# Gate rows' transposes moved behind the product with v, into its banks, and the gate products of two half-batches put in one turn

## Chip, cores and metric

One Trainium2 chip, one of its cores. The metric is the device time of one execution in microseconds (us); lower is better. The kernel is one launch that holds attention and the mixture of experts.

## What is computed

Causal attention in a window of 64 positions, followed by a mixture of experts that picks one expert for each token and skips the tokens whose skip score isn't positive:

```python
scores = scale * np.matmul(q, k.transpose(0, 1, 3, 2))        # B=8, H=8, S=576, D=64
rel = pos[:, None] - pos[None, :]
scores = np.where((rel >= 0) & (rel < 64), scores, -1000000000.0)
attn = softmax(scores)
out = np.matmul(attn, v)                                      # [8, 8, 576, 64]
x = out.transpose(0, 2, 1, 3).reshape(B * S, H * D)           # [4608, 512]
do_compute = x @ w_skip > 0
logits = x[do_compute] @ w_gate                               # 8 experts
e_idx = argmax(logits); gate_w = softmax(logits)[e_idx]
y = gate_w * (relu(x @ w1[e_idx]) @ w2[e_idx])                # 512 -> 1024 -> 512
out = x, with x + y in the rows of do_compute
```

## The kernel before

**Attention tiles.** The 4608 tokens are worked in 36 tiles of 128 rows, each of two blocks of 64 positions. A batch has nine blocks; four tiles take eight of them, and after each second batch a ninth tile takes the two last blocks of both (a "tail tile", tile number 8 of each nine). A block looks at its own 64 positions and at the 64 before. A half-batch `n` (0 to 15) is four blocks, two tiles; its v with the columns around it is the buffer `vm`, whose first tile is `first_of[n] = 9*(n//4) + 2*(n%4)`.

**A turn.** The order of the instructions is written out by hand: a loop `for t in range(NT - 1)` issues one turn for each tile, and each engine works through its own queue in that order. Turn t starts the loads of its table, then issues:
- `score(t + 1)`: on PE four matmuls of the band mask (L238) and 16 small products of q and k (L252) into `ps` (the trace counts each product of fp32 operands twice);
- the gate work of its table `gate_at`: `gate_v` multiplies `vT` (v transposed) with the gate's and the skip's weights `wg`, so that the logits come out of the attention's own product (PE L336, `pw`, four matmuls; ACT L338 copies it to `vw`); a turn later `gate_vt` turns `vw` back with two transposes (PE L344, `pk`), ACT L356 copies them beside v in columns 65 to 74 of `vm`, and POOL L357 copies the upper half of `vm` to the slot of the block before. `gate_tail` and `gate_tail_t` do the same for the tail tiles with one transpose;
- `soften(t)`: DVE takes the maximum (L271) and subtracts it (L272), ACT the exponential (L277);
- `tile_out(t - 2)`, and in it `av_tile`: the product with v (PE L388, 16 matmuls, 74 columns a head: 64 of v, the row sum, nine of the gate) into two PSUM banks `av`; then DVE takes the reciprocal of the sums (`r`, L399, L400), writes `x` (L401) and the gate's columns `lh` (L407);
- `transpose_p(t - 1)`: eight PE transposes `pt` (L285), which ACT copies to `ptm` (L286) for the product of the next turn;
- `lower`: ACT copies of one block of `vm` (L364).

So a product of turn t is that of tile t - 2, and a half-batch's `vm` is first used in turn `first_of[n] + 2`.

**PSUM.** `pw`, `pk` and `pt` take turns in two banks (tag "t", `bufs=2`). `ps` has two buffers of two banks, `av` one of two banks (`bufs=1`), of which the product takes columns 0 to 295 of each.

**Routing beside it.** From the gate's columns of eight or six tiles at a time, generators that `routes(1)` steps three times a turn work out the lists of tokens for each expert. Most of it is POOL: the logits' sums (`lh`, `lg`, L468, L469), the choice (`gd` to `gohb`, L484 to L502), the rank in the expert's list (`gs`, `gds`, `rows`, L505, L537 to L539) and the lists' entries as one-hot rows (`xg`, L599 to L611). Two small products on PE, the ranks' (L517, L520) and the lists' (L560), are written into the `av` banks behind the product's columns, from column `PRAT` = 320 on; DVE reads the ranks' (`gds`, L530). POOL's copies of L357 stand in the same queue.

**Loads.** SP issues them in program order, a few turns ahead: `load_v(n)`, `vT` and then `vm` of the same half-batch, in turn `first_of[n] - 4` (L296, L302); q and k at `first_of[n] - 5` (L210, L211); the attention's outputs `x` go out between them (L426).

**Experts.** After the last tile, tokens are gathered by an indirect DMA (L732) and the experts' products (L918 to L920) run to the end.

Of the kernel before, what the change touches and what calls it, by code (L numbers as in the profile page):

```python
# [8 lines left out]
F32 = mybir.dt.float32  # L9
# [11 lines left out]
P = 128  # L21
# [29 lines left out]
AHEADQ, AHEADV = 5, 4  # L51
# [17 lines left out]
XN = max(n for _, n, _ in ITEMS)  # L69
NEG = -float(2**36)  # L70
VW = 64 + 1 + 9
PRAT = 320


def token_tiles():
# [69 lines left out]
def window_attention_moe(ctx: ExitStack, tc, a, out):  # L145
# [147 lines left out]
    def load_vT(n):  # L293
        b, g = divmod(n, 2)
        vT = vtp.tile([P, 4, 256], F32, name="vT")
        nc.sync.dma_start(vT, a["vT"][b, g])  # L296
        vTs[n] = vT
# [8 lines left out]
            nc.gpsimd.memset(vm[:64, 0], 0.0)  # L306
        vms[n] = vm

    def load_v(n):
        load_vT(n)  # L310
        load_vm(n)

    vTs, vws = {}, {}

    def load_v_tail(m):
# [23 lines left out]
        return vw  # L339

    def gate_t(vw, nt):
        pk = psum.tile([P, nt, P], F32, name="pk", tag="t", bufs=2, padded_shape=[P, 4, P])
        for j in range(nt):
            nc.tensor.transpose(pk[:, j], vw[:, j * P : j * P + P], ident)  # L344
        return pk.rearrange("p n (h c) -> p n h c", c=16)[..., 0:9]

    def gate_v(n):
        vws[n] = gate(vTs.pop(n), 2)

    def gate_vt(n):  # L350

        b, g = divmod(n, 2)
        vm = vms[n]
        pg = gate_t(vws.pop(n), 2)
        w = vm.rearrange("p (j z) h c -> p j z h c", z=2)
        nc.scalar.copy(w[:, :, 1, :, 65:74], pg)  # L356
        nc.gpsimd.tensor_copy(w[64:, :, 0], w[:64, :, 1])  # L357
        for j in range(2):
            vs[9 * (n // 4) + 2 * (n % 4) + j] = [vm[:, 2 * j], vm[:, 2 * j + 1]]

# [8 lines left out]
    def gate_tail_t(m):  # L369
        vt, vw = vms["t", m]  # L370
        pg = gate_t(vw, 1)
        for z in range(2):
            nc.scalar.copy(vt[64:, z, :, 65:74], pg[64 * z : 64 * z + 64, 0])
        vs[9 * m + 8] = [vt[:, 0], vt[:, 1]]

    def tail_lower(m, z):
# [2 lines left out]
    def av_tile(t, lh, sums, av=None):  # L379
        blks = tiles[t]  # L380
        ptm, win = pts.pop(t), vs.pop(t)
        x = xp.tile([P, D], F32, name="x", bufs=XPB)
        if av is None:
            av = pav.tile([P, 2, 512], F32, name="av")
        banks["av"] = av
        for h in range(8):
            for hf in range(2):
                nc.tensor.matmul(  # L388
                    av[64 * hf : 64 * hf + 64, h // 4, (h % 4) * VW : (h % 4 + 1) * VW],
                    ptm[:, (h % 2) * 4 + h // 2, 64 * hf : 64 * hf + 64],  # L390
                    win[hf][:, h],
                    start=True,
                    stop=True,
                )
        if sums:
            sums()
        r = sm.tile([P, 2, 4], F32, name="r")
        src = av[:, :, : 4 * VW].rearrange("p z (h c) -> p z h c", c=VW)
        nc.vector.tensor_scalar(r, src[..., 64], 1e-9, None, op0=ALU.add)  # L399
        nc.vector.reciprocal(r, r)  # L400
        pace[0] = nc.vector.tensor_tensor(  # L401
            x.rearrange("p (z h c) -> p z h c", z=2, c=64),
            src[..., 0:64],
            r.unsqueeze(3).to_broadcast([P, 2, 4, 64]),
            op=ALU.mult,
        )
        nc.vector.tensor_tensor(  # L407
            lh.rearrange("p c (z h) -> p z h c", z=2),
            src[..., 65:74],
            r.unsqueeze(3).to_broadcast([P, 2, 4, 9]),  # L410
            op=ALU.mult,
        )
        if sums:
            sums()
        stores.append((x, blks))
        while len(stores) > (SDELAY if t < NT - 6 else 0):
            store()
# [362 lines left out]
    def listing():  # L780
        step(later, held2)

    grp = [0, 0, None]
    heads = [sum(GRP[:i]) for i in range(len(GRP))]

    def tile_out(t, av=None):
        if t in heads:
            n = GRP[heads.index(t)]
            grp[:] = [t, n, xp.tile([P, n, 9, H], F32, name="lh")]
        t0, n, lh = grp  # L790
        behind = None
        if held[0] == "sums" and held[1] >= WAIT.get(t0, 2):
            behind = sums
        elif held2[0] == "lists" and held2[1] >= LWAIT:
            behind = listing
        av_tile(t, lh[:, t - t0], behind, av)
        progress[0] = t + 1
        if t + 1 == t0 + n:
            late.append(route(t0, n, lh))
# [337 lines left out]
    with tc.manual_schedule():  # L1137
# [17 lines left out]
        def when_at(t, f, n):  # L1155
            at.setdefault(max(t, 0), []).append((f, n))

        gate_at, lower_at = {}, {}
        for n in range(NG):
            if n >= 2:  # L1160
                when_at(first_of[n] - AHEADQ, load_qk, n)
                when_at(first_of[n] - AHEADV, load_v, n)
            gt = max(first_of[n] - (1 if n < NSLOW else 2), 0)
            gate_at.setdefault(gt, []).append((gate_v, n))
            at_t = gt + 1
            gate_at.setdefault(at_t, []).append((gate_vt, n))
            lower_at.setdefault(at_t, []).append((lower, n, 1))
            if n % 2:
                lower_at.setdefault(at_t + 1, []).append((lower, n, 0))
        for m in range(B // 2):  # L1170
            when_at(9 * m + 4, load_qk_tail, m)
            when_at(9 * m + 2, load_v_tail, m)
            lower_at.setdefault(9 * m + 4, []).append((tail_lower, m, 0))
            lower_at.setdefault(9 * m + 7, []).append((tail_lower, m, 1))
            gate_at.setdefault(9 * m + 5, []).append((gate_tail, m))
            gate_at.setdefault(9 * m + 6, []).append((gate_tail_t, m))
        keep_busy(12)
        score(0)
        keep_busy(4)
        for t in range(NT - 1):  # L1180
            m, r = divmod(t, 9)
            for f, n in at.get(t, ()):
                f(n)
            score(t + 1)
            gates = gate_at.get(t, ())
            if t > 1:
                for f, n in gates:
                    f(n)
            routes(1)
            soften(t)  # L1190
            if t >= BOTH:
                drip()
            if t == 0:
                for f, n in gates:
                    f(n)
            if t >= 2:
                tile_out(t - 2)
            drip()
            routes(1)
            if t >= 1:  # L1200
                transpose_p(t - 1)
            if t == 1:
                for f, n in gates:
                    f(n)
            if t == 1:
                clear_rows()
            if t == 3:
                load_constants()
            if t == 5:
                set_constants()  # L1210
            routes(1)
            for f, n, j in lower_at.get(t, ()):
                f(n, j)
            for _ in range(U0.count(t)):
                weight_dma_first()
            if t >= NT - 3:
                weight_hi(t + 3 - NT)
# [268 lines left out]
```

## Time and profile before

| what | value |
|---|---|
| median of 3 runs | 415.93 us (414.9 to 416.22) |
| the profiled execution | 417.13 us, its span 415.4 us |
| granted TensorE clock over the span | 0.995 of 2.4 GHz |
| busy: PE, DVE, ACT, POOL | 392.6, 301.7, 216.7, 159.6 us (95, 73, 52, 38% of the span) |
| DMA | 99.41 MB, 239 GB/s on the mean |
| attention, and experts | the first to about 160 us, the second from there to 415 us |

The span is the time from the first to the last instruction that the profiler records; the execution is 1.73 us longer. "Busy" is time in which an engine works; idle time of one engine says nothing until it is known who waits for whom. In a timeline row, a bracket names the idle time in front of the instruction and the instruction that ended it.

### The profile page before, as it was taken

The numbers are of one execution on the slowest core, as the hardware profiler recorded it, in microseconds if no ns is written. First come the engines' busy times: TensorE is split into PE (matmuls) and PEld (weight loads), VectorE is DVE, ScalarE is ACT, GpSimd is POOL, SyncE is SP. The second block draws the span as 40 slices with busy tenths as digits, with TensorE's granted clock in tenths as the row PEclk, the third lists the DMA queues.
The fourth block names the chain that finished last, engine by engine and source line by source line (L and its number), as shares of the span: only waits on it lengthen the run. The fifth ranks groups of instructions, "written<-read, shape, count | busy, mean of one in ns | idle before, by whom it ended". The sixth has DMA issues, their size and how long they took to land.

```text
span 415.4 us, 11519 instructions
## 1 busy us (share of the span) xinstructions
PE 392.6 (95%) x4623; PEld 327.6 (79%) x4623; DVE 301.7 (73%) x547; ACT 216.7 (52%) x373; POOL 159.6 (38%) x296
## 2 busy tenths in 40 slices
PE   8898999999999898989999999999999999999794
PEld 3576787877878677879988798898898889988673
DVE  3586899899799795999468789565455486658871
ACT  2675877767677694536224445244335345533450
POOL 1521268567958878477204114022024030100110
PEclk9999999999999998999999999999999999999999
DMA  8999999999995694866605777645136886741510
GB/s 279 408 336 386 405 361 377 411 395 300 394 412 186 212 358 145 234 230 194 224 0 175 255 271 216 225 170 174 55 134 208 266 259 211 245 157 52 184 48 21
DMA packets 35096, 99.41 MB, mean 239 GB/s; under 512 B 4480, under 2 KB 5888, under 8 KB 35040
## 3 DMA queue, kind: packets, MB, share of 16 engines
q1 hardware_dynamic: 30560, 87.22, 60.1%
q0 software_dynamic: 3200, 9.58, 6.5%
q10 hardware_dynamic: 1280, 1.85, 1.2%
q8 instruction: 37, 0.61, 0.6%
q14 instruction: 19, 0.16, 0.1%
HBM read 84.57 MB, written 14.39 MB: 238 GB/s over the span
## 4 chain that ended last, share of the span: by engine, by line
PE 64%; issue 13%; DMA 10%; DVE 4%; POOL 4%; ACT 3%; POOLq 0%; ACTq 0%; SPq 0%; another core or an unknown queue 0%; DVEq 0%
PE av L388 8%; PE pt L285 7%; PE p L918 6%; PE ps L252 5%; PE p L919 5%; PE p L920 5%; DMA out<-yo,les 5%; PE yv L918 3%; PE yv L919 3%; PE yv L920 3%; PE ps L238 2%; PE pw L336 2%; PE yw L919 2%; PE yw L918 2%; PE yw L920 2%
## 5 line engine op out<-in xcount | busy, mean ns | idle before, releaser
L852 DVE TENSOR_TENSOR wlo<-raw,whi 128x1024 fp32r<-128x1024 f32 x70 | 86.3, 1244 | 15.9 <-ACT whi L848 14.2
L1022 POOL DMA_INDIRECT out<-yo,les x18 | 17.6, 976 | 147.7 <-DVE yo L1013 138.0
L982 ACT ACTIVATE hh<-p 128x256 fp32r<-128x256 f32 (+4 forms) x56 | 22.9, 410 | 98.3 <-PE p L920 84.5
L848 ACT CAST whi<-raw 128x1024 fp32r<-128x1024 f32 x72 | 74.2, 1046 | 0.0
L918 PE MATMUL p<-xp,whi 128*128 128x256 f32 (+4 forms) x192 | 58.2, 303 | 0.4 <-ACT xp L896 0.4
L919 PE MATMUL p<-xp,whi 128*128 128x256 f32 (+4 forms) x192 | 57.1, 297 | 0.2 <-DVE xp L899 0.2
L920 PE MATMUL p<-xp,wlo 128*128 128x256 f32 (+4 forms) x192 | 56.8, 296 | 0.0
L985 DVE SCALAR_TENSOR_TENSOR hl<-p,hh 128x256 fp32r<-128x256 f32 (+4 forms) x56 | 25.2, 451 | 43.5 <-ACT hh L982 28.0
L277 ACT ACTIVATE s<-s 128x1024 f32<-128x1024 f32 x36 | 38.1, 1059 | 31.8 <-DVE s L272 31.7
L271 DVE TENSOR_REDUCE mx<-ps 128x8 f32<-128x1024 f32 x36 | 43.6, 1211 | 6.7 <-PE ps L252 6.7
L272 DVE TENSOR_TENSOR s<-ps,mx 128x1024 f32<-128x1024 f32 x36 | 44.1, 1225 | 4.6
L388 PEld LDWEIGHTS av<-vm,ptm 128*64 128x64 f32 x992 | 34.7, 136 | 13.3 <-issue 6.2
L388 PE MATMUL av<-vm,ptm 128*64 128x74 f32 x992 | 39.8, 230 | 4.2 <-issue 1.7
L286 ACT COPY ptm<-pt 128x512 f32<-128x512 f32 x72 | 38.2, 581 | 8.2 <-PE pt L285 8.0
L285 PE MATMUL pt<-ident,s 128*128 128x128 f32 x288 | 39.9, 282 | 0.0
L918 PEld LDWEIGHTS p<-xp,whi 128*128 128x128 f32 x192 | 36.2, 188 | 3.0 <-ACT xp L896 0.7
L919 PEld LDWEIGHTS p<-xp,whi 128*128 128x128 f32 x192 | 36.2, 188 | 1.2 <-DVE xp L899 0.5
L920 PEld LDWEIGHTS p<-xp,wlo 128*128 128x128 f32 x192 | 36.1, 188 | 0.0
L252 PE MATMUL ps<-k,q 64*64 64x128 f32 x1024 | 33.6, 270 | 1.5 <-DMA q<-qT 1.5
L285 PEld LDWEIGHTS pt<-ident,s 128*128 128x128 f32 x288 | 31.6, 143 | 2.5 <-issue 0.3
L252 PEld LDWEIGHTS ps<-k,q 64*64 64x64 f32 x1024 | 30.0, 133 | 4.3 <-issue 2.3
L357 POOL COPY vm<-vm 64x1184 f32<-64x1184 f32 x16 | 18.6, 1166 | 31.9 <-ACT vm L356 26.7
(243 smaller groups left out, 819.4 us busy)
## 6 DMA issues: line engine op xcount, KB each, us to landing
raw<-wq SPq DMA_DIRECT2D x72, 512.0 KB
vm<-vp SPq DMA_DIRECT2D x15, 592.0 KB
vT<-vT SPq DMA_DIRECT2D x16, 512.0 KB
out<-x SPq DMA_DIRECT2D x32, 256.0 KB
q<-qT SPq DMA_DIRECT2D x14, 512.0 KB
k<-kT SPq DMA_DIRECT2D x7, 640.0 KB
k<-kT SPq DMA_DIRECT2D x7, 512.0 KB
kt<-kT SPq DMA_DIRECT2D x8, 256.0 KB
```

Of the source, the lines that this page charges most:

```text
L252: nc.tensor.matmul(ps[64 * hf : 64 * hf + 64, r, p], q[h, p], k[h, :, p], start=False, stop=p == 3, skip_group_check=True,)
L271: nc.vector.tensor_reduce(mx, flat, axis=AX.X, op=ALU.max)
L272: pace[0] = nc.vector.tensor_tensor(s, flat, mx.unsqueeze(2).to_broadcast([P, 8, P]), op=ALU.subtract)
L277: nc.scalar.activation(s, s, AF.Exp, scale=0.125)
L285: nc.tensor.transpose(pt[:, p], s[:, 4 * r + p], ident)
L286: nc.scalar.copy(ptm[:, 4 * r : 4 * r + 4], pt)
L388: nc.tensor.matmul(av[64 * hf : 64 * hf + 64, h // 4, (h % 4) * VW : (h % 4 + 1) * VW], ptm[:, (h % 2) * 4 + h // 2, 64 * hf : 64 * hf + 6 ...
L848: nc.scalar.copy(ring[n % RING][0], raw_of[n])
L852: by.tensor_tensor(lo, raw_of[n], hi.bitcast(F32), op=ALU.subtract)
L918: nc.tensor.matmul(o, lh, rh, start=first, stop=False, skip_group_check=parts)
L919: nc.tensor.matmul(o, lh, rl, start=False, stop=False, skip_group_check=parts)
L920: nc.tensor.matmul(o, ll, rh, start=False, stop=last, skip_group_check=parts)
```

## The change

The gate's transposes go out of the banks of tag "t": they are written into the two `av` banks of the turn's product, from column `GAT` = 368 on, behind the product's 16 matmuls (`turned_at`, called from `av_tile`). Their copies on ACT and POOL are kept in a list and issued at the end of the turn, behind `transpose_p`. To make room, `PRAT` becomes 296. From half-batch 4 on, the gate product of an odd `n` is issued in the turn of the even one before it, and its `vT` is loaded two turns earlier, right behind `vm` of the even one. The lists' product isn't issued in a turn that has transposes behind its product. The tail tile's transpose of the first two batches moves from turn 6 to turn 7.

```diff
--- before.py
+++ after.py
@@ -69,7 +69,8 @@
 XN = max(n for _, n, _ in ITEMS)
 NEG = -float(2**36)
 VW = 64 + 1 + 9
-PRAT = 320
+PRAT = 296
+GAT = 368
 
 
 def token_tiles():
@@ -306,10 +307,6 @@
             nc.gpsimd.memset(vm[:64, 0], 0.0)
         vms[n] = vm
 
-    def load_v(n):
-        load_vT(n)
-        load_vm(n)
-
     vTs, vws = {}, {}
 
     def load_v_tail(m):
@@ -339,13 +336,15 @@
         return vw
 
     def gate_t(vw, nt):
-        pk = psum.tile([P, nt, P], F32, name="pk", tag="t", bufs=2, padded_shape=[P, 4, P])
+        pk = banks["av"][:, 2 - nt :, GAT : GAT + P]
         for j in range(nt):
             nc.tensor.transpose(pk[:, j], vw[:, j * P : j * P + P], ident)
         return pk.rearrange("p n (h c) -> p n h c", c=16)[..., 0:9]
 
     def gate_v(n):
         vws[n] = gate(vTs.pop(n), 2)
+
+    kept = []
 
     def gate_vt(n):
 
@@ -353,8 +352,12 @@
         vm = vms[n]
         pg = gate_t(vws.pop(n), 2)
         w = vm.rearrange("p (j z) h c -> p j z h c", z=2)
-        nc.scalar.copy(w[:, :, 1, :, 65:74], pg)
-        nc.gpsimd.tensor_copy(w[64:, :, 0], w[:64, :, 1])
+
+        def keep():
+            nc.scalar.copy(w[:, :, 1, :, 65:74], pg)
+            nc.gpsimd.tensor_copy(w[64:, :, 0], w[:64, :, 1])
+
+        kept.append(keep)
         for j in range(2):
             vs[9 * (n // 4) + 2 * (n % 4) + j] = [vm[:, 2 * j], vm[:, 2 * j + 1]]
 
@@ -369,8 +372,12 @@
     def gate_tail_t(m):
         vt, vw = vms["t", m]
         pg = gate_t(vw, 1)
-        for z in range(2):
-            nc.scalar.copy(vt[64:, z, :, 65:74], pg[64 * z : 64 * z + 64, 0])
+
+        def keep():
+            for z in range(2):
+                nc.scalar.copy(vt[64:, z, :, 65:74], pg[64 * z : 64 * z + 64, 0])
+
+        kept.append(keep)
         vs[9 * m + 8] = [vt[:, 0], vt[:, 1]]
 
     def tail_lower(m, z):
@@ -392,6 +399,8 @@
                     start=True,
                     stop=True,
                 )
+        for f, n in turned_at.get(t + 2, ()):
+            f(n)
         if sums:
             sums()
         r = sm.tile([P, 2, 4], F32, name="r")
@@ -780,6 +789,7 @@
     def listing():
         step(later, held2)
 
+    turned_at = {}
     grp = [0, 0, None]
     heads = [sum(GRP[:i]) for i in range(len(GRP))]
 
@@ -791,7 +801,7 @@
         behind = None
         if held[0] == "sums" and held[1] >= WAIT.get(t0, 2):
             behind = sums
-        elif held2[0] == "lists" and held2[1] >= LWAIT:
+        elif held2[0] == "lists" and held2[1] >= LWAIT and t + 2 not in turned_at:
             behind = listing
         av_tile(t, lh[:, t - t0], behind, av)
         progress[0] = t + 1
@@ -1159,11 +1169,12 @@
         for n in range(NG):
             if n >= 2:
                 when_at(first_of[n] - AHEADQ, load_qk, n)
-                when_at(first_of[n] - AHEADV, load_v, n)
+                when_at(first_of[n] - AHEADV - (2 if n > NSLOW and n % 2 else 0), load_vT, n)
+                when_at(first_of[n] - AHEADV, load_vm, n)
             gt = max(first_of[n] - (1 if n < NSLOW else 2), 0)
-            gate_at.setdefault(gt, []).append((gate_v, n))
             at_t = gt + 1
-            gate_at.setdefault(at_t, []).append((gate_vt, n))
+            gate_at.setdefault(gt if n < NSLOW or n % 2 == 0 else first_of[n - 1] - 2, []).append((gate_v, n))
+            turned_at.setdefault(at_t, []).append((gate_vt, n))
             lower_at.setdefault(at_t, []).append((lower, n, 1))
             if n % 2:
                 lower_at.setdefault(at_t + 1, []).append((lower, n, 0))
@@ -1173,7 +1184,8 @@
             lower_at.setdefault(9 * m + 4, []).append((tail_lower, m, 0))
             lower_at.setdefault(9 * m + 7, []).append((tail_lower, m, 1))
             gate_at.setdefault(9 * m + 5, []).append((gate_tail, m))
-            gate_at.setdefault(9 * m + 6, []).append((gate_tail_t, m))
+            turned_at.setdefault(9 * m + (6 if m else 7), []).append((gate_tail_t, m))
+        assert max(map(len, turned_at.values())) == 1
         keep_busy(12)
         score(0)
         keep_busy(4)
@@ -1202,6 +1214,11 @@
             if t == 1:
                 for f, n in gates:
                     f(n)
+                banks["av"] = pav.tile([P, 2, 512], F32, name="av")
+                for f, n in turned_at.get(t, ()):
+                    f(n)
+            while kept:
+                kept.pop(0)()
             if t == 1:
                 clear_rows()
             if t == 3:
```

What becomes of the queues' order by it, in three places.

**SP, the loads of turns 5 to 7, before.** `vT_539` and `vm_541` are those of half-batch 4, `vT_701` and `vm_703` those of half-batch 5; k and q between them belong to half-batch 5 too, and `out<-x` are stores.

```order
L296 DMA vT_539<-vT 128x1024
L302 DMA vm_541<-vp 128x2x592
L426 DMA out<-x_421 128x512
L210 DMA k1_107<-kT 128x1280
L211 DMA q_625<-qT 128x1024
L426 DMA out<-x_500 128x512
L296 DMA vT_701<-vT 128x1024
L302 DMA vm_703<-vp 128x2x592
```

And now, with `vT_537` and `vm_539` of half-batch 4, `vT_542` and `vm_696` of half-batch 5:

```order
L297 DMA vT_537<-vT 128x1024
L303 DMA vm_539<-vp 128x2x592
L297 DMA vT_542<-vT 128x1024
L435 DMA out<-x_420 128x512
L211 DMA k1_107<-kT 128x1280
L212 DMA q_625<-qT 128x1024
L435 DMA out<-x_494 128x512
L303 DMA vm_696<-vp 128x2x592
```

The second `vT` has moved ahead of a store, k, q and another store; it stands right behind `vm` of half-batch 4.

**POOL, turns 21 to 24, before.** The list entries of tiles 8 to 15 (`vals` to `xg`) and in their middle the copy of half-batch 10's `vm` (`vm_1613`):

```order
L592 CAST vals_82<-gl3_1891 128x8
L357 COPY vm_1613<-vm_1613 64x2x592
L599 TENSOR_TENSOR xg5_120<-cf_76,gc_1881 128x256
L600 TENSOR_SCALAR xg5_120<-xg5_120 128x256
L603 TENSOR_SCALAR xg8_123<-cf_76,gk_1885 128x128 x8
L611 TENSOR_TENSOR xg6_121<-xg5_120,vals_82 128x640
L611 TENSOR_TENSOR xg7_122<-xg5_120,vals_82 128x640
L306 MEMSET vm_2059 64x592
L357 COPY vm_1786<-vm_1786 64x2x592
```

And now, where that `vm` is `vm_1601`:

```order
L608 TENSOR_TENSOR xg5_120<-cf_76,gc_1877 128x256
L609 TENSOR_SCALAR xg5_120<-xg5_120 128x256
L612 TENSOR_SCALAR xg8_123<-cf_76,gk_1881 128x128 x8
L620 TENSOR_TENSOR xg6_121<-xg5_120,vals_82 128x640
L620 TENSOR_TENSOR xg7_122<-xg5_120,vals_82 128x640
L358 COPY vm_1601<-vm_1601 64x2x592
L307 MEMSET vm_2047 64x592
L477 TENSOR_TENSOR lh_1632<-lh_1632 128x54x4
L477 TENSOR_TENSOR lh_1632<-lh_1632 128x54x2
```

The copy has moved behind the twelve instructions that build `xg`; the next one (`vm_1786` before) stands behind `lg` now.

**POOL, turns 26 to 28, before.** The ranks of the third group and the copy of half-batch 12's `vm` (`vm_2059`):

```order
L505 TENSOR_SCALAR gs_2304<-gs_2304 128x6
L357 COPY vm_2059<-vm_2059 64x2x592
L537 TENSOR_TENSOR gds_2387<-gds_2387,gohb_2302 128x48
L468 TENSOR_TENSOR gds_2387<-gds_2387 128x6x4
L468 TENSOR_TENSOR gds_2387<-gds_2387 128x6x2
L469 TENSOR_TENSOR rows_83<-gds_2387 128x6
L539 TENSOR_TENSOR rows_83<-rows_83,gnd_2297 128x6
L626 TENSOR_SCALAR ckey_2410<-base_80 128x8
```

And now, where it is `vm_2047`:

```order
L514 TENSOR_SCALAR gs_2297<-gs_2297 128x6
L546 TENSOR_TENSOR gds_2377<-gds_2377,gohb_2295 128x48
L477 TENSOR_TENSOR gds_2377<-gds_2377 128x6x4
L477 TENSOR_TENSOR gds_2377<-gds_2377 128x6x2
L478 TENSOR_TENSOR rows_83<-gds_2377 128x6
L548 TENSOR_TENSOR rows_83<-rows_83,gnd_2290 128x6
L358 COPY vm_2047<-vm_2047 64x2x592
L635 TENSOR_SCALAR ckey_2402<-base_80 128x8
```

The copy has moved from ahead of `gds` to behind `rows`, ahead of all that follows from the ranks.

## Rows read from the trace of the kernel before

**Rows 1.** Windows: us, busy of PE, PEld, DVE, ACT, POOL; PEclk, DMA share, GB/s

```profile
36.00:50.00 14.00, 13.95 (x289) 11.19 (x287) 12.45 (x22) 11.05 (x20) 2.92 (x3) 1.00 1.03 399
64.00:78.00 14.00, 14.00 (x291) 11.40 (x287) 12.72 (x23) 10.63 (x21) 12.53 (x25) 1.00 1.03 398
...
160.00:162.00 2.00, 2.00 (x15) 1.85 (x12) 1.26 (x4) 0.58 (x1) 1.92 (x3) 0.54 0.06 23
```

**Rows 2.** PE timeline, turns 20 to 23: start, us, engine, line, op

```profile
93.44 1.07 PE L285 MATMUL pt<-ident,s 128*128 128x128 f32 x8
...
94.68 1.04 PE L252 MATMUL ps<-k,q 64*64 64x128 f32 x32
95.66 0.44 PE L344 MATMUL pk<-ident,vw 128*128 128x128 f32 x2
96.02 1.26 PE L388 MATMUL av<-vm,ptm 128*64 128x74 f32 x32
97.21 1.09 PE L285 MATMUL pt<-ident,s 128*128 128x128 f32 x8
98.23 0.41 PE L238 MATMUL ps<-band,identb 64*64 64x512 bf16 x4
98.47 1.04 PE L252 MATMUL ps<-k,q 64*64 64x128 f32 x32
99.44 0.64 PE L336 MATMUL pw<-vT,wg 128*32 128x256 f32 x8
100.01 1.25 PE L388 MATMUL av<-vm,ptm 128*64 128x74 f32 x32
...
103.81 0.42 PE L336 MATMUL pw<-vTt,wg 128*32 128x128 f32 x8
104.16 1.26 PE L388 MATMUL av<-vm,ptm 128*64 128x74 f32 x32
```

**Rows 3.** DVE and ACT timelines, turns 9 to 10

```profile
49.61 0.17 DVE L399 TENSOR_SCALAR r<-av 128x8 f32<-128x8 f32 x1 [0.24 <-PE av L388]
...
52.25 0.29 ACT L356 COPY vm<-pk 128x144 f32<-128x144 f32 x1 [0.83 <-POOL lh L468]
53.41 1.06 ACT L277 ACTIVATE s<-s 128x1024 f32<-128x1024 f32 x1 [0.86 <-DVE s L272]
54.37 1.05 ACT L286 COPY ptm<-pt 128x512 f32<-128x512 f32 x2
```

**Rows 4.** PE timeline, turns 6 and 7

```profile
35.94 0.55 PE L344 MATMUL pk<-ident,vw 128*128 128x128 f32 x3
36.42 1.26 PE L388 MATMUL av<-vm,ptm 128*64 128x74 f32 x32
...
39.84 0.64 PE L336 MATMUL pw<-vT,wg 128*32 128x256 f32 x8
40.41 1.25 PE L388 MATMUL av<-vm,ptm 128*64 128x74 f32 x32
```

**Rows 5.** Waits of SP's queue from 39 to 41.2 us: us, times, longest

```profile
SPq L210 <- DMA vm<-vp: 0.8, 1, 0.8
```

**Rows 6.** SP timeline, turns 5 to 7

```profile
33.66 0.38 SPq L302 DMA_DIRECT2D vm<-vp  x1
...
40.33 0.33 SPq L210 DMA_DIRECT2D k<-kT  x1
```

**Rows 7.** POOL timeline, turns 20 to 24

```profile
95.10 0.30 POOL L537 TENSOR_TENSOR gds<-gds,gohb 128x64 f32<-128x64 f32 x1 [2.01 <-DVE gds L530]
...
99.22 1.17 POOL L357 COPY vm<-vm 64x1184 f32<-64x1184 f32 x1
...
109.03 0.58 POOL L306 MEMSET vm<- 64x592 f32 x1
```

**Rows 8.** PE and DVE timelines, turns 24 to 26

```profile
107.84 1.25 PE L388 MATMUL av<-vm,ptm 128*64 128x74 f32 x32
...
112.41 0.20 DVE L482 TENSOR_REDUCE gmx<-lg 128x6 f32<-128x48 f32 x1 [1.94 <-POOL lg L469]
...
115.16 0.41 PE L238 MATMUL ps<-band,identb 64*64 64x512 bf16 x4 [0.54 <-DVE s L272]
...
116.85 0.44 PE L344 MATMUL pk<-ident,vw 128*128 128x128 f32 x2 [0.41 <-ACT ptm L286]
```

**Rows 9.** POOL and PE timelines, turns 26 to 31

```profile
120.55 0.27 POOL L537 TENSOR_TENSOR gds<-gds,gohb 128x48 f32<-128x48 f32 x1 [0.47 <-DVE gds L530]
...
137.22 1.16 POOL L357 COPY vm<-vm 64x1184 f32<-64x1184 f32 x1
138.44 1.25 PE L388 MATMUL av<-vm,ptm 128*64 128x74 f32 x32 [1.43 <-POOL vm L357]
```

**Rows 10.** POOL and PE timelines, turns 33 and 34

```profile
145.96 1.17 POOL L357 COPY vm<-vm 64x1184 f32<-64x1184 f32 x1
...
153.63 1.56 PE L388 MATMUL av<-vm,ptm 128*64 128x74 f32 x32 [0.92 <-ACT ptm L286]
...
157.84 2.44 PE L388 MATMUL ps<-vm,ptm 128*64 128x74 f32 x32 [1.46 <-ACT ptm L286]
```

**Rows 11.** DVE timeline, turn 20

```profile
93.62 0.17 DVE L399 TENSOR_SCALAR r<-av 128x8 f32<-128x8 f32 x1 [0.38 <-PE av L520]
...
97.69 0.15 DVE L399 TENSOR_SCALAR r<-av 128x8 f32<-128x8 f32 x1
...
101.35 0.16 DVE L399 TENSOR_SCALAR r<-av 128x8 f32<-128x8 f32 x1
```

## Prediction

> **What bounds the kernel now.** I read the windows first, then PE's timeline turn by turn, then who ends PE's few idle times. In two windows of attention [rows 1] PE is busy for 13.95 and 14.00 of 14 us at the full granted clock, with DVE at 12.45 and 12.72 and the DMA engines fully used (share 1.03, 399 GB/s). So a turn lasts as long as PE's instructions in it, DVE is about a tenth behind, and a load that is asked for earlier gets its place only at another load's cost. PE's idle times that I found between turns 24 and 31 are short ones behind DVE and ACT [rows 8] and 1.43 us behind a POOL copy [rows 9]: there POOL's routing sets the pace. From 164 us on the experts keep PE busy, so a delay at the end of attention is passed on whole.
>
> **PE's share, worked out.** From start to start [rows 2]: eight `pt` 1.02 (97.21 to 98.23; 0.128 each), mask and scores 1.21 (98.23 to 99.44), a gate product 0.57 (99.44 to 100.01), two gate transposes 0.36 (95.66 to 96.02), the product with v 1.19. The tail's gate product, half as wide, takes 0.35 (103.81 to 104.16): 0.22 for the columns and some 0.13 for the change to the next kind of work.
> - Transposes behind the product stand ahead of eight more of their kind, so I price them like those: 2 x 0.128 = 0.26, 0.10 less than now.
> - The first of two gate products in a row is not followed by another kind of work: 0.44, 0.13 less.
> - Nine turns now take 9 x 3.42 (without gate work) + 4 x 0.57 + 4 x 0.36 + 0.35 + 0.26 = 35.1. Then they take 9 x 3.42 + 2 x (0.44 + 0.57) + 0.35 + 4 x 0.26 + 0.13 = 34.3. PE would save 0.8 in nine turns.
>
> **What is given back.** The next product overwrites the banks in which the transposes lie, so it must wait for ACT's copy of them; that copy now stands behind the exponential and both `ptm` copies in ACT's queue. From `r` to the exponential of the next turn DVE takes 3.80 (49.61 to 53.41), and from there both `ptm` copies end 2.01 later (55.42); the copy of the transposes adds 0.29 [rows 3]: 6.10 from one `r` to the product two turns on. Before, ACT made that copy long ahead (52.25), and nobody waited for it. With the product's 1.19 two turns can't be shorter than some 7.3, or 7.6 where transposes stand ahead of `r` as well. Two turns with a gate transpose and no gate product on PE alone would be shorter than that; when I walk nine turns with both limits, two of them (turns 0 and 4 of each nine) become 4.02 long where PE would need 3.67. That is 0.7 of the 0.8. **Term: -0.1 in nine turns.**
>
> **One-off on PE.** In turn 6 transposes of 0.48 stood ahead of the product (35.94 to 36.42) [rows 4] and now stand behind it: products from there on are 0.48 earlier. **Term: -0.48.** In a turn with two gate products the product comes 0.56 later in its turn than now: it counts where the routing starts from such a turn (turn 20).
>
> **A new wait on a load.** Half-batch 5's gate product now stands in turn 7, two turns earlier. Its turn began at 39.84 [rows 4]; with turn 6 shorter by 0.22 and the first product's 0.44, the second would start at 39.84 - 0.22 + 0.44 = 40.06. Its `vT` is issued behind `vm` of half-batch 4 (issued at 33.66), and that transfer was complete only at 40.33, where SP had waited 0.8 for it [rows 5, 6]. 512 KB at 399 GB/s are another 1.31. So it is there at about 41.5, and PE, which works in order, stands for 1.4. Behind it wait the product, the transposes and so DVE and ACT. Bounds: 0, if it overtakes the `vm`; 1.6, if it starts only at 40.33. I take 1.4, since everything before it is in one saturated queue. The later pairs (turns 11, 16, 20, ...) have more than two turns' lead of their half-batch's loads; I price them at 0, with up to 0.5 each as the other end. **Term: +1.4.** SP itself issues the load two rows earlier; k and q move back by 1.31 and are needed three turns later: nothing.
>
> **POOL.** A copy of `vm` takes 1.17 [rows 7]. It used to be issued in mid-turn; now it stands at the turn's end and in two places falls behind other routing work.
> - Half-batch 10: the copy stood inside the list work at 99.22; now it comes behind the last `xg`. That work runs without a pause from `gds` at 95.10 to 109.03 [rows 7]: 13.93, without the copy and its gap 12.69. The start follows turn 20, which is late by -0.48 - 0.2 (turns 6 to 20) + 1.4 + 0.56 = 1.26 or so. So 95.10 + 1.26 + 12.69 + 1.24 = 110.3 for the product that needs it, in place of 107.84 [rows 8]: +2.45. Of this DVE's wait of 1.94 for `lg`, which isn't later than now, gives back what PE idled behind it, 0.54 + 0.41 [rows 8]: +1.5 at turn 26.
> - Half-batch 12: its copy ran in time that POOL idled before `gds` (0.47 left) [rows 9]; now it stands behind `gds` and `rows`, ahead of the chain that runs without a pause to the copy at 137.22, for which the product at 138.44 waits (1.43). +1.24 on that chain. **Together: +2.7 at turn 31.**
> - Half-batch 15: the copy goes from ahead of the first gathers (145.96) to behind them. The product that needs it waits for ACT, not for POOL [rows 10]: nothing, or up to 0.1 later. The gathers come 1.2 earlier, but PE's idle times there end with ACT's `ptm`: nothing.
>
> **Sum.** -0.48 - 0.2 + 1.4 + 0.56 = +1.26 at turn 20; POOL makes it +1.5 at turn 26 and +2.75 at turn 31; passed on to the end. Against the profiled execution of 417.13 that is 419.9; that one lies 1.2 above the median of the three runs, 415.93, against which I give **418.7**.
>
> **Rivals.**
> - *A, the saving comes through (chance 0.12).* ACT copies in time, so nothing is given back: from turn 6 to 26, -0.8 x 20 / 9 = -1.8, and -0.48. For: ACT is busy 11 of 14 us [rows 1]. It needs `vT` in time, and it decides where `lg` and not the copy of half-batch 10 sets turn 24. Then turn 26 is at -1.5 to -2.2, half-batch 12 adds 1.24, the last turns save another 0.6: about -1.3, **414.6**. Against: [rows 3] and the unbroken list work [rows 7].
> - *B, no wait for the load (0.22).* It lands by 40.1, or the delay is absorbed at turn 24. Turn 20 is then at -0.1, half-batch 10 is ready at +1.1, less 0.95: +0.15 at turn 26, +1.4 at turn 31, of which the earlier gathers can give back up to 1.2: 416.1 to 417.3, I say **416.7**, no difference that can be told.
> - *C, the clock falls (0.15).* PE's idle time in turn 31 grows from 1.43 to some 2.7. The one fall in attention came after idle times of 0.92 and 1.46 [rows 10]: a granted clock of 0.54 from 160 to 162 [rows 1], the lower of its two levels (1.2 GHz) for most of it. A second such stretch of some 3.4 us costs half of it: +1.7, **420.4**.
> - *D, DVE is held by the banks (0.06).* In turn 20, where the ranks' small products stand behind the product in its banks, `r` waits 0.38 for the last of them [rows 11], though it reads other columns. With transposes there, `r` starts 0.26 later in 20 turns (16 half-batches and 4 tails). My walk has it in the 7.6 alone, since DVE's own round is 3.66 (97.69 to 101.35) [rows 11] and turns are longer; if it were on the path in 16 of them: +4.2, **423**.
>
> The Trainium skill, "PSUM — Partial Sum Buffer", section "PSUM bank collisions raise a hardware error", says that two engines must be kept apart by bank and group of 32 partitions, not by address. By that rule this change has a price that columns alone don't show: DVE, ACT and PE now share the product's banks in one turn, and what was free in another bank is put in a row. The 0.38 agrees. By the rule alone, with no slack anywhere, the sum would be that of D.
>
> **The numbers.** About 0.3%, 1.25 us, is what a measurement of this kernel can tell from no change. My forecast has 0.45; with C and D that makes 0.66 slower, B 0.22 the same, A 0.12 faster. The range goes from 415.0, under B and its bounds, to 421.5, above C; A and D, 0.18, are left out.
>
> **What would show it.** Right: PE idle by 1.4 in turn 7, ended by the DMA of `vT`; the product of turn 24 at about 110 with an idle time behind POOL's copy; the product of turn 31 at about 141, behind the copy; turns of about 4.0 behind ACT's copy of the transposes. Two transposes behind the product of 0.26, the first gate product of two of 0.44. Wrong: no idle time in turn 7 (B), turns that keep to 3.67 and nine turns of 34.3 (A), a granted clock of 0.5 near turn 31 (C), DVE without slack and `r` each time waiting for the transposes (D). If the product of turn 31 isn't late although the copy of half-batch 12 stands where I say, POOL's chain is not what I took it for.

## The result, and the profile after

The change makes the kernel slower: 421.9 us median of 6 runs (420.47 to 424.45) against 416.12 (414.9 to 417.8) of the kernel before. The ratio is 1.0147, with an interval of 1.0121 to 1.0173: 5.0 to 7.2 us, 6.1 in the middle. Forecast were 418.7, +2.8, in a range that ends at 421.5: the direction was right, the size was less than half of it, and the median lies 0.4 above the range.

The profiled execution took 420.94 us, its span 419.2. The same windows as in [rows 1], and one more, of the kernel after (us, busy of PE, PEld, DVE, ACT, POOL; PEclk, DMA share, GB/s):

```profile
36.00:50.00 14.00, 11.91 (x253) 9.63 (x249) 10.33 (x19) 9.69 (x18) 1.17 (x1) 1.00 1.03 384
64.00:78.00 14.00, 13.49 (x291) 11.14 (x293) 13.12 (x26) 10.94 (x20) 11.48 (x26) 1.00 1.02 387
140.00:144.00 4.00, 1.21 (x40) 0.97 (x34) 1.98 (x2) 2.31 (x4) 3.78 (x6) 1.00 0.40 112
144.00:148.00 4.00, 4.00 (x48) 3.40 (x48) 2.66 (x7) 1.58 (x3) 2.67 (x8) 0.57 0.82 256
```

PE, which had no pause in the first two windows, now idles 2.1 and 0.5 us of 14. From 140 to 144 us it stands, while POOL works; right behind it the granted clock falls to 0.57. The main pauses of PE's timeline after, from turn 6 to the end of attention:

```profile
36.07 1.26 PE L395 MATMUL av<-vm,ptm 128*64 128x74 f32 x32
...
39.71 0.64 PE L333 MATMUL pw<-vT,wg 128*32 128x256 f32 x8
41.73 0.64 PE L333 MATMUL pw<-vT,wg 128*32 128x256 f32 x8 [1.38 <-DMA vT<-vT]
42.30 1.25 PE L395 MATMUL av<-vm,ptm 128*64 128x74 f32 x32
...
46.61 1.25 PE L395 MATMUL av<-vm,ptm 128*64 128x74 f32 x32 [0.71 <-issue]
47.80 0.44 PE L341 MATMUL av<-ident,vw 128*128 128x128 f32 x2
48.07 1.04 PE L286 MATMUL pt<-ident,s 128*128 128x128 f32 x8
...
57.65 1.07 PE L333 MATMUL pw<-vT,wg 128*32 128x256 f32 x16
58.65 1.26 PE L395 MATMUL av<-vm,ptm 128*64 128x74 f32 x32
...
86.00 1.25 PE L395 MATMUL av<-vm,ptm 128*64 128x74 f32 x32 [0.22 <-ACT vm L357]
...
103.00 1.25 PE L395 MATMUL av<-vm,ptm 128*64 128x74 f32 x32 [0.75 <-POOL xg L608]
112.03 1.25 PE L395 MATMUL av<-vm,ptm 128*64 128x74 f32 x32 [1.55 <-POOL vm L358]
124.91 1.25 PE L395 MATMUL av<-vm,ptm 128*64 128x74 f32 x32 [0.49 <-ACT vm L357]
143.19 1.25 PE L395 MATMUL av<-vm,ptm 128*64 128x74 f32 x32 [2.79 <-POOL vm L358]
157.07 1.25 PE L395 MATMUL av<-vm,ptm 128*64 128x74 f32 x32 [0.87 <-ACT vt L378]
160.46 1.56 PE L395 MATMUL av<-vm,ptm 128*64 128x74 f32 x32 [1.12 <-ACT ptm L287]
163.46 1.61 PE L395 MATMUL ps<-vm,ptm 128*64 128x74 f32 x32 [0.24 <-ACT ptm L287]
...
166.90 1.25 PE L395 MATMUL ps<-vt,ptm 128*64 128x74 f32 x32
```

The first rows answer to [rows 4]: the wait for the second `vT`, 1.38 us, is there as forecast, and the products come 1.89 us late in turn 7 (42.30 for 40.41). The rows at 47.80 and 57.65 answer to [rows 2]: two transposes behind the product take 0.27 and two gate products in a row 1.00, which is what I had priced (0.26 and 1.01). The products of turns 24 and 31 wait for POOL's copy, 1.55 and 2.79 us, where [rows 8, 9] had none and 1.43. And there are waits for copies on ACT at the turn's end, L357 and L378 (L356 and L373 before). The row at 166.90 is the last product with v; the experts follow it.

How late a product is against the kernel before, read off PE's timelines of this and of the runs below (us; each one profiled execution, a minus is earlier):

| turn | after | e2 | e3 | e5 | e7 | e9 | e11 |
|---|---|---|---|---|---|---|---|
| 6 | -0.35 | -0.09 | -1.82 | -2.02 | -0.54 | -2.34 | -1.85 |
| 8 | 2.29 | 1.89 | -0.68 | 2.34 | 0.28 | 0.13 | -1.22 |
| 23 | 2.62 | 2.07 | -0.68 | 2.93 | 0.09 | 0.45 | -1.41 |
| 24 | 4.19 | 2.07 | 0.56 | 3.02 | 0.05 | 1.97 | -1.45 |
| 26 | 3.27 | 2.38 | -0.53 | 2.82 | -0.12 | 1.05 | -1.62 |
| 31 | 4.75 | 2.46 | 0.52 | 2.96 | 0.11 | 2.46 | -1.40 |
| 34 | 7.01 | 2.46 | 2.33 | 3.60 | 0.75 | 3.46 | -1.39 |
| last | 5.62 | 2.42 | 1.55 | 2.82 | 0.03 | 2.13 | -1.47 |

Up to turn 6 executions differ by up to 2 us through events that change with the execution (below); from turn 8 on the differences between rows of a column are in the main the edit's, though falls of the clock come into them too. The last row is against 161.28: the kernel before has its last product at 162.88, and its profiled execution lost 1.6 us at half clock between turns 36 and 37 ([rows 1]; 5.04 from one product to the next, 3.44 in e2, e7 and e10, whose clock didn't fall there). For this reason the two spans differ by 3.8 us only. Most of the 7.01 of turn 34 that is gone in the last row was given back in turns 35 and 36, where PE waits for ACT's `ptm` in either kernel: 0.92 and 1.46 us before [rows 10], 1.12 and 0.24 after.

### The profile page after: what moved, and what is told of

Same layout as the page of the kernel before. It is cut to its first block, busy times and chain, and to the rows that moved or that the text cites. A ratio compares the mean times of both kernels' runs of the same rounds, so it can differ in the third digit from the quotient of the medians.

```text
span 419.2 us, 11522 instructions
## 1 busy us (share of the span) xinstructions
PE 390.8 (93%) x4623; PEld 329.3 (79%) x4623; DVE 302.5 (72%) x547; ACT 216.2 (52%) x373; POOL 160.7 (38%) x296
## 3 DMA queue, kind: packets, MB, share of 16 engines
q10 hardware_dynamic: 1280, 1.85, 1.2%
## 4 chain that ended last, share of the span: by engine, by line
PE 39%; issue 18%; DMA 16%; POOL 12%; DVE 9%; ACT 3%; POOLq 1%; ACTq 0%; SPq 0%; DVEq 0%
DMA out<-yo,les 5%; PE p L928 4%; PE p L929 4%; PE p L930 4%; PE av L395 4%; DMA vT<-vT 4%; DMA q<-qT 4%; POOL xg L620 2%; PE yv L928 2%; POOL xg L612 2%; DMA raw<-wq 2%; PE yw L928 2%; PE yv L929 2%; PE yw L929 2%; PE yw L930 2%
## 5 line engine op out<-in xcount | busy, mean ns | idle before, releaser
L286 PEld LDWEIGHTS pt<-ident,s 128*128 128x128 f32 x288 | 33.3, 146 | 1.1 <-issue 0.2
```

Of the source, the lines that this page charges most:

```text
L286: nc.tensor.transpose(pt[:, p], s[:, 4 * r + p], ident)
```

## Experiments

Each ratio is to the kernel before, timed beside it; "us" is what the ratio exceeds 1 by, times 416.

**One part alone.** e1 has the transposes behind the product, with their copies, but no pairs; e2 has the pairs and the early `vT` alone; e3 is the kernel before with POOL's copy alone put where the change has it; e4 is the change without the first pair.

```diff
# e1, against the change
-  when_at(first_of[n] - AHEADV - (2 if n > NSLOW and n % 2 else 0), load_vT, n)
+  when_at(first_of[n] - AHEADV, load_vT, n)
-  gate_at.setdefault(gt if n < NSLOW or n % 2 == 0 else first_of[n - 1] - 2, []).append((gate_v, n))
+  gate_at.setdefault(gt, []).append((gate_v, n))
# e3, against the kernel before; kept is emptied behind transpose_p
-  nc.gpsimd.tensor_copy(w[64:, :, 0], w[:64, :, 1])
+  kept.append(lambda: nc.gpsimd.tensor_copy(w[64:, :, 0], w[:64, :, 1]))
# e4, against the change
-  when_at(first_of[n] - AHEADV - (2 if n > NSLOW and n % 2 else 0), load_vT, n)
+  when_at(first_of[n] - AHEADV - (2 if n > NSLOW + 2 and n % 2 else 0), load_vT, n)
-  gate_at.setdefault(gt if n < NSLOW or n % 2 == 0 else first_of[n - 1] - 2, []).append((gate_v, n))
+  gate_at.setdefault(gt if n < NSLOW + 2 or n % 2 == 0 else first_of[n - 1] - 2, []).append((gate_v, n))
```

e2 makes the two edits that e1 takes back to the kernel before.

> The transposes, their copies and the lists' product as in the change; gate products and loads of vT in the turns of before. Theory (the +5.8 us are a sum: 1.4 us wait for vT and 0.7 behind it on ACT, some 0.5 per nine turns from waits for ACT's copy of the transposes, 2.5 from the two POOL copies that stand later, and a stretch at half clock): without the 2.1 of the load and without the 0.8 that pairs save, +3.5 to +5 against before, product of turn 31 waits over 2 us for POOL. Rival (the early load is the cost): +1 or less.

Measured: ratio 1.0063 (1.004 to 1.0085), +2.6. Less than the theory's +3.5, more than the rival's +1. PE's wait in turn 31 was 2.57 us behind POOL.

> Pairs of gate products and the early vT alone; transposes and copies in place and banks of before. Theory: PE waits 1.4 us for vT in turn 7, 0 to 0.7 more behind ACT, six pairs give back 0.13 each; POOL's chain starts that much later and takes up to 0.9 of it: 0 to +1.5. Rival (the early load is the cost): +3 or more.

Measured: 1.0049 (1.0032 to 1.0065), +2.0: above the theory's +1.5, below the rival's +3. The wait for `vT` was 1.46. Its column shows why it is more than that: 1.89 in turn 8, and from there to turn 31 nothing is given back; the delay even grows by 0.6, though the pairs leave PE less to do. POOL's chain took nothing of it.

> The kernel before, with only POOL's copies of vm issued at the turn's end, behind the transposes, where the change has them. Theory: half-batch 10 costs 1.2 of which 0.95 comes back, half-batch 12 costs 1.24 at turn 31 (PE idle there 2.5 us or more): +1.5, and +3.2 if the clock falls behind that idle time. Rival (POOL's queue has slack): within 0.5 of before.

Measured: 1.0048 (1.0018 to 1.0079), +2.0, between the theory's two figures. In its column turn 24 adds 1.24, turn 26 gives 1.09 back, turn 31 adds 1.05, and behind that turn its clock fell (0.5 from 139.2 to 142.6 us), which added 1.6 up to turn 32. Place and price, with what the clock lost behind the pause, belong to POOL's order alone, since nothing else is edited. The waits:

```profile
108.40 1.25 PE L390 MATMUL av<-vm,ptm 128*64 128x74 f32 x32 [1.17 <-POOL vm L359]
...
138.96 2.08 PE L390 MATMUL av<-vm,ptm 128*64 128x74 f32 x32 [2.48 <-POOL vm L359]
```

> The change, but half-batches 4 and 5 are not paired, so vT of 5 is loaded and used as before; pairs from 6 and 7 on. Theory: the 1.4 us for vT and the 0.7 behind ACT in turn 8 are gone, and with them about 2 of the 5.8: +3.5 to +4.3 against before. Rival (the delay is taken up where POOL makes PE wait anyway, turn 24 and 31): the same as the change, +5 to +6.

Measured: 1.012 (1.0091 to 1.0149), +5.0. Its middle lies between the theory's +4.3 at most and the change's 6.1, and the intervals overlap: this one alone doesn't decide. PE still idles 0.91 in turn 8, without any load that is late; so the 0.71 of the change needs no late load.

**POOL put back.** e5 is the change with POOL's copy in two: the 65 columns of v at the old place, the gate's nine by ACT.

```diff
+  def shift_v(n):                       # in gate_at, turn at_t
+      w = vms[n].rearrange("p (j z) h c -> p j z h c", z=2)
+      nc.gpsimd.tensor_copy(w[64:, :, 0, :, 0:65], w[:64, :, 1, :, 0:65])
 def keep():
     nc.scalar.copy(w[:, :, 1, :, 65:74], pg)
-    nc.gpsimd.tensor_copy(w[64:, :, 0], w[:64, :, 1])
+    nc.scalar.copy(w[64:, :, 0, :, 65:74], w[:64, :, 1, :, 65:74])
```

> The change, but POOL copies only the 65 columns of v, at the place in the turn that it had before, and ACT moves the nine gate columns to the upper half behind its copy of the transposes. Theory (POOL's order costs about 0.4 at turn 24, 1.3 at turn 31 and part of a stretch at half clock): 2 to 3 us of the change's 6.1 go, +3 to +4; no wait for POOL over 1.5 us in turn 31. Rival (POOL only takes the place of other waits): +5.5 or more.

Measured: 1.0054 (1.0035 to 1.0073), +2.2: better than the theory. The change loses 3.9 us of its 6.1 with this one edit. The edit is a little more than the old order: POOL's copy takes 1.06 in place of 1.17 us and no longer waits for ACT's copy of the transposes. Order alone is e3's +2.0, and e1 to e7 (below) 2.1. Turn 24 no longer waits, and turn 31 waits for POOL as long as before the change:

```profile
141.40 1.25 PE L399 MATMUL av<-vm,ptm 128*64 128x74 f32 x32 [1.45 <-POOL vm L351]
```

**The copy out of the banks by DVE.** e6 is e5 with `nc.vector.tensor_copy(w[:, :, 1, :, 65:74], pg)` right behind `lh` in place of ACT's copy.

> As e5_split_copy, and the transposes are copied out of the banks by DVE right behind lh, not by ACT at the turn's end. Theory (products wait for ACT's queue in turns 15, 18, 22, 27 and others): another 1 to 2 us go, +1.5 to +3. Rival (DVE is as near to its limit as ACT, 0.3 more each time): no better than e5_split_copy, or worse.

Measured: 1.0067 (1.0044 to 1.0089), +2.8, no better than e5: the rival holds. The products no longer wait for L357, and arrive no earlier: from turn 8 to 31 its products fall back by another 1.0 us (2.21 to 3.22), e5's by 0.6. The rival's reason fits the rows, without being tried by itself: a turn with transposes and no gate product needs 3.67 on PE, DVE's own round 3.66 [rows 11] and the copy on top.

**Transposes without pairs, POOL as before.** e7 is e1 with e5's edit, e8 is e6's edit on top.

> e1_transposes_only with the split copy of e5_split_copy: transposes behind the product, no pairs, no early load, POOL as before. Theory (of e1's +2.6 some 2 are POOL's order): 0 to +1. Rival (the banks are the cost): +2 or more.

Measured: 1.0013 (0.9988 to 1.0038), +0.5. The transposes in the product's banks, with their copies, cost nothing that can be told, and bring nothing: from turn 8 to 23 products gain 0.19 where PE's work alone would give 7 x 0.1.

> e7_transposes_split with DVE's copy in place of ACT's. Theory (waits for ACT taken away, PE saves 0.1 in 16 turns and 0.2 in turn 6): -1 to +0.3. Rival (DVE's added 0.3 makes turns longer): +0.5 or more.

Measured: 1.0005 (0.9982 to 1.0029), +0.2; between theory and rival, and not to be told from e7.

**The load.** e9 is the change with `vT` of the pair's second half-batch loaded ahead of the first one's `vm`.

```diff
-  when_at(first_of[n] - AHEADV - (2 if n > NSLOW and n % 2 else 0), load_vT, n)
+  if n < NSLOW or n % 2 == 0:
+      when_at(first_of[n] - AHEADV, load_vT, n)
+      if n >= NSLOW:
+          when_at(first_of[n] - AHEADV, load_vT, n + 1)
   when_at(first_of[n] - AHEADV, load_vm, n)
```

> The change, with the second vT of a pair loaded ahead of the first half-batch's vm instead of behind it; all else as in the change, POOL's order too. Theory (the wait for vT, 1.38, and ACT's queue held by the second gate product's copy, 0.7 in turn 8, are paid in full): no wait for a DMA in turn 7, about 2 us of 6.1 gone, +4. Rival (most of it comes back later, as e4's +5.0 suggests): +5 or more.

Measured: 1.0087 (1.006 to 1.0115), +3.6, as the theory says in size; not in both of its details:

```profile
39.58 0.64 PE L333 MATMUL pw<-vT,wg 128*32 128x256 f32 x8 [0.64 <-DMA vT<-vT]
44.45 1.25 PE L395 MATMUL av<-vm,ptm 128*64 128x74 f32 x32 [0.71 <-issue]
```

The load is 2.15 us earlier (39.58 for 41.73) and still 0.64 late, as this execution had reached turn 7 earlier. The 0.71 in turn 8 stayed.

**The ends.** e10 is e7 with half-batch 15 and the last tail tile turned and copied as before the change; e11 also the first tail tile, in turn 6.

```diff
+  def old_way(n, tail=0):
+      return n in ((15,), (0, 3))[tail]     # e10: ((15,), (3,))
-  turned_at.setdefault(at_t, []).append((gate_vt, n))
+  (gate_at if old_way(n) else turned_at).setdefault(at_t, []).append((gate_vt, n))
...
+  if old: pk = psum.tile([P, nt, P], F32, name="pk", tag="t", bufs=2, padded_shape=[P, 4, P])
+  if old_way(n): keep()                     # at once; else kept.append(keep)
```

> e7_transposes_split, with the last half-batch (15) and the last tail tile turned and copied as before (bank of tag t, at once). Theory (in turns 33 and 34 products wait 0.52 and 0.29 us for copies that stand at the turn's end): 0.6 to 0.8 less than e7, -0.3 to 0 against before. Rival (ACT sets the end of attention anyway): as e7, +0.5.

Measured: 1.0002 (0.9983 to 1.0022), +0.1, in the middle 0.4 less than e7; the intervals overlap. The two waits of e7 in turns 33 and 34 are gone from the trace, and products of turn 34 that were late by 0.75 are late by 0.13. e7's rows, on PE and on ACT, show what they were:

```profile
146.92 1.25 PE L399 MATMUL av<-vm,ptm 128*64 128x74 f32 x32 [0.52 <-issue]
150.81 1.26 PE L399 MATMUL av<-vm,ptm 128*64 128x74 f32 x32 [0.29 <-ACT vt L382]
```

```profile
145.59 1.05 ACT L287 COPY ptm<-pt 128x512 f32<-128x512 f32 x2
146.53 0.30 ACT L361 COPY vm<-av 128x144 f32<-128x144 f32 x1
...
149.23 1.05 ACT L287 COPY ptm<-pt 128x512 f32<-128x512 f32 x2
150.31 0.45 ACT L382 COPY vt<-av 64x72 f32<-64x72 f32 x2
```

Each product starts right at the end of the copy that stands behind both `ptm` copies. But neither wait reaches the end of attention. Turn 35, turn 36 and the last product, in e7 and then in e10:

```profile
154.21 1.57 PE L399 MATMUL av<-vm,ptm 128*64 128x74 f32 x32 [1.11 <-ACT ptm L287]
157.87 1.61 PE L399 MATMUL ps<-vm,ptm 128*64 128x74 f32 x32 [0.90 <-ACT ptm L287]
161.31 1.26 PE L399 MATMUL ps<-vt,ptm 128*64 128x74 f32 x32
```

```profile
153.75 1.57 PE L411 MATMUL av<-vm,ptm 128*64 128x74 f32 x32 [1.07 <-ACT ptm L287]
157.91 1.61 PE L411 MATMUL ps<-vm,ptm 128*64 128x74 f32 x32 [1.41 <-ACT ptm L287]
161.35 1.25 PE L411 MATMUL ps<-vt,ptm 128*64 128x74 f32 x32
```

The product of turn 31 stands at 138.55 and 138.56 in the two, the last at 161.31 and 161.35: what e7 loses in turns 33 and 34 it gets back in turn 36, where it waits 0.90 in place of 1.41 for ACT's `ptm`. That is the rival's reason, that ACT sets the end of attention.

> e10_end_as_before, and the first tail tile's transpose too in turn 6 as before. Theory (the tail's copies in turn 7 stand ahead of the copy that turn 8's product waits for, 0.9 us): product of turn 8 at least 0.4 earlier than in e7, another 0.4 off. Rival (loads set the time up to turn 8): as e10.

Measured: 0.998 (0.9959 to 1.0002), -0.8, the lowest of all kernels here; its interval just takes in no change. The product of turn 8 comes at 43.10, 1.5 earlier than in e7, but e7 was 1.3 behind already in turn 6. Against e1, which reaches turn 6 when e11 does (34.51 and 34.57) and has the tail's copies in turn 7, it comes 0.86 earlier. PE still idles 0.82 ahead of it. ACT's queue shows for what:

```profile
40.29 1.06 ACT L278 ACTIVATE s<-s 128x1024 f32<-128x1024 f32 x1 [0.65 <-DVE s L273]
41.26 1.05 ACT L287 COPY ptm<-pt 128x512 f32<-128x512 f32 x2
42.32 0.68 ACT L380 COPY vm<-vm 64x592 f32<-64x592 f32 x1
```

This is `lower`, whose block the product of turn 8 reads; it follows DVE's `s`, the exponential and `ptm`. Where PE gets there sooner, it waits for it. The tail's copies ahead of `lower` lengthen that wait; they aren't all of it.

> All of it: the change with the split copy (e5), vT ahead of vm (e9) and both ends as before (e11). Theory: what is left are the pairs themselves, whose second product puts 0.56 more into one turn and saves 0.13 of PE time: e11 with a difference of 0 to +0.5. Rival (pairs pay once no wait is left): below e11 by 0.5 or more.

Measured: 1.0012 (0.9989 to 1.0035), +0.5: 1.3 above e11 in the middle, against the rival that pairs pay. The difference has an uncertainty of 1.3, and part of the profiled execution are pauses without any releaser (the last section), so how much the pairs themselves cost stays open, somewhere from 0 to 2.6.

## Why the prediction fell short

The runs divide the 6.1 us. Putting POOL's copies back takes away 3.9 (the change to e5), unpairing and with it the early load 1.7 (e5 to e7), the first and last turns 1.4 (e7 to e11), and -0.8 is left. Each of these differences has an uncertainty of 1.3 to 1.4 us; the first two are clear of it, the third isn't.

The profiled execution of the change gives its own account: its products are 2.6 us late in turn 23, 2.1 more up to turn 31, 1.6 more through half clock behind that turn, and 0.7 of it is given back by the last product: 5.6. Forecast were 1.3 up to turn 20, 1.5 for POOL, and nothing for the rest. So three steps of the forecast failed: the gain of 0.48 in turn 6 with the -0.2 behind it, the size of POOL's term, and the clock, which stood outside the sum.

- **PE's own work: right.** 0.27 for two transposes, 1.00 for two gate products.
- **What is given back: right in kind, too small.** From turn 10 to turn 19 products need 36.27 us (53.67 to 89.94) where the kernel before needs 35.91 (52.10 to 88.01), with the same products of the routing in both. Forecast was 0.1 less, it is 0.36 more. Products that wait for L357 are the cause I named, with 0.2 to 0.5 in single turns; they aren't all of it. e6, which takes these waits away by a copy on DVE, isn't faster.
- **The wait for `vT`: right,** 1.38 for 1.4. It was right too that the delay isn't taken up: e2 keeps all of it to the end.
- **-0.48 in turn 6: failed.** "Products from there on are 0.48 earlier" left out `lower`, ACT's copy of the block that the product of turn 8 reads. Its row and the product's, of the kernel before:

```profile
43.54 0.68 ACT L364 COPY vm<-vm 64x592 f32<-64x592 f32 x1
44.32 1.25 PE L388 MATMUL av<-vm,ptm 128*64 128x74 f32 x32
```

  From the start of `lower` to that product it is 0.78 us. It is 0.78 or 0.79 in every other kernel here too, but for e2 with 0.83. So the product of turn 8 stood at the end of `lower` before the change already, and what PE saves ahead of it becomes idle time: 0.71 in the change, 0.25 (e12) to 1.12 (e8) in the runs where no load was late. `lower` follows DVE's `s`, the exponential and `ptm`; in the change the tail's copies stand ahead of it as well (0.44). Where the load is late, its landing sets turn 7 (the second gate product starts at 41.66 to 41.85 in the change, e2, e5 and e6, whenever they reached turn 6), and a gain ahead of it is lost there. My first explanation after the result, that ACT's queue was held by the late load, fell with e4.
- **POOL: places right, size wrong.** "+1.5 at turn 26 and +2.75 at turn 31". In the trace turn 24 adds 1.57 (1.19 forecast), turn 26 gives back 0.92 (0.95), turn 31 adds 1.48 (1.24): 2.1 for 1.5. The price of POOL's order in the runs is 2.0 (e3), 2.1 (e1 to e7) and 3.9 (the change to e5), each to about 1.3, the clock's part within it.
- **The clock: left out of the sum.** I had put it into a rival with a chance of 0.15, as if it came or not; it is a price on the mean. The kernel before has a mean granted clock of 0.989 to 0.991 (88 executions, timed beside the runs). Those with POOL's copies late have 0.984 to 0.988: e1 and e4 0.984, the change and e3 0.987, e9 0.988; the eight other runs have 0.990 to 0.994. On the mean the four runs are 0.003 below the kernel timed beside them, and 0.003 of 416 us at full clock is 1.2 us, an estimate. In the profiled executions the clock fell right behind turn 31 in three of these five (the change, e3, e4) and in none of the nine others. The price shows in turn 32 of e9, where the clock held, and of the change, where it fell (its turn 31 is at 143.19, above): with pauses of 2.72 and 2.79 the next product comes 4.15 and 5.76 us later. That the clock makes up the rest of POOL's price wasn't tried by itself. First e9, then the change:

```profile
140.90 1.26 PE L395 MATMUL av<-vm,ptm 128*64 128x74 f32 x32 [2.72 <-POOL vm L358]
145.05 1.25 PE L395 MATMUL av<-vm,ptm 128*64 128x74 f32 x32
```

```profile
148.95 1.26 PE L395 MATMUL av<-vm,ptm 128*64 128x74 f32 x32
```

- **The ends: right in sum, wrong in the turns.** "Nothing, or up to 0.1 later" for half-batch 15 looked at POOL alone, and I had left the last turns out of the walk. Copies at the turn's end make products of turns 33 and 34 wait, 0.52 and 0.29 in e7, 0.87 in the change; but by the last product that is made up, since ACT's `ptm` sets the end of attention. It stands 22.8 us behind that of turn 31 in e7, e10 and e11 alike, and in the kernel before without its half clock. What e11 gains on e7 would then come from the first tail tile; by the ratios it isn't clear of noise.
- **The rivals.** A and B are out: without the wait in turn 7 the change is still 5.0 slower (e4), with 0.64 of it left 3.6 (e9). D, DVE held by the banks in every turn, is out by e7: the same transposes in the same banks, +0.5. C came true in the change's profiled execution; it was no rival but a part of the sum.

The rule of the Trainium skill that I weighed ("PSUM — Partial Sum Buffer", "PSUM bank collisions raise a hardware error"), that engines must be kept apart by bank, is seen here as waits. In the list of all waits from 36 to 160 us of the kernel after (us in total, times, longest) `r` is held by the transposes:

```profile
DVE r L408 <- PE av L341: 6.2, 6, 2.4
```

These are six waits in a stretch that has transposes in 17 turns; the longest, 2.4, is in the turn with the late load. With e7 at +0.5 they can't have cost PE much; the price by the rule alone, +4.2, didn't come.

## What to carry to other kernels

An instruction that moves in the program moves in the queue of each engine that it uses: here two POOL copies, off PE's path by themselves, fell behind long routing work and cost about 2 us or more, while the transposes without them cost nothing that can be told (e7). A saving on the busiest engine should be followed to the next place where another engine's copy sets the time, in the first and last turns too: here one copy on ACT took the gain of turn 6, and another gave back the waits of the last turns. Where a new idle time of the matrix engine is forecast, the mean loss through the clock behind it belongs in the sum.

## What was not expected of the hardware

- PE pauses that nothing in the profile ends, in the middle of one group of matmuls: 1.69 us in turn 5 of the kernel before and 1.70 in e2, 0.57 after, none in e3, though PE's work up to there is the same in the kernel before, e2 and e3. In e12, 1.62 us in turn 24:

```profile
108.00 0.49 PE L253 MATMUL ps<-k,q 64*64 64x128 f32 x9
110.11 0.88 PE L253 MATMUL ps<-k,q 64*64 64x128 f32 x23 [1.62 <-issue]
```

  They come and go with the execution; what PE waits for there stays open.
- The granted clock fell to half for 3.41 us early in turns 2 to 3 in the profiled executions of the change, e4, e6, e7, e8 and e10, and not in the others, though the work up to there is almost the same; it makes products some 1.5 us later, and much of that is taken up by turn 8. With the pauses above it is the reason why single executions differ by up to 2 us in turn 6, and why the verdicts above rest on the ratios.
